# Fetching the next short group's row numbers and tokens one slot earlier in the expert stage of an attention and mixture-of-experts kernel

## The chip, the cores and the metric

The program runs on one core of a Trainium2 chip. The metric is device microseconds of one execution. Launches are timed singly; the kernel before was run three times. Beside them one execution was taken by the hardware profiler, and all rows below are from that one.

## The reference, cut to what matters

Three blocks run one after the other: attention with a learned position bias, a token and channel mixer, and a mixture of eight experts in which every token goes to one expert. Only the last block is touched.

```python
# x: [2, 576, 512] after the first two blocks; 8 experts; F = 1024
logits = x @ w_gate
e = argmax(logits) where the local gate is low (or at token 0), else the expert of the token before
p = softmax(logits)
h = maximum(x[b, s] @ w1[e], 0.0)          # w1[e]: 512 x 1024
out[b, s] = p[e] * (h @ w2[e])             # w2[e]: 1024 x 512
```

## The kernel before, in words

The 1152 tokens are sorted by expert on the chip. For each expert, rows of a table in HBM (`meta`) hold the row number of a token and its weight p. The tokens of an expert are worked in full slots of 128 (8 slots, t = 0 to 7) and what is left over, at most 32 tokens, in a short group (`little`, k = 0 to 3). A full slot does its two matrix products in three passes of float32r halves (`mm1`, `mm2`, line 743), for which the weights, loaded as float32 into `raw`, are split into a high part by ScalarE (a cast, line 1327) and a low part by VectorE or GpSimd (line 1328); of every four chunks the last one's low part is GpSimd's. A short group does the same with plain float32 matmuls of 32 columns against its own copies of the weights (`lw1`, `lw2`).

The short group k is worked between the steps of slots 2k and 2k+1, by a table of parts that `beside_slots` (lines 1506 to 1522) fills and `run` calls: its token transpose (`little_T`, line 1431) at the "top" of slot 2k, its first product (`little_mm1`, line 1441) at the end of slot 2k, its second transpose (line 1450) in the middle of slot 2k+1, its second product (line 1460) at the end of slot 2k+1. "Middle" is after the first half of the slot's `mm2`, the token transpose of slot t+2 (`x_T`, line 1335), the last two weight splits of slot t+2's `w1` and the issue of the weights of slot t+3. "Top" is in the loop's next turn, between the two halves of the next slot's `mm1`.

What one fetch for a short group, `little_tokens(k)`, issues, in order:

- on ScalarE's queue, a register load of the group's first row and a DMA (line 1400) of 32 rows of `meta`, repeated four times over the partitions, into `lmt` (line 1400). For k = 0 this is on SyncE's queue;
- on GpSimd, a tensor_scalar (line 1402) that makes four addresses of each row number (`lat`), which waits for `lmt`;
- on GpSimd, an indirect DMA (line 1404) that gathers the tokens' 128-element quarters from `x2d` into `lxt`, which waits for `lat`.

`lmt`, `lat` and `lxt` have two buffers each, so groups k and k+1 have different ones. `little_T` waits for `lxt`. All engines take their instructions in order; SyncE issues all weight loads, ScalarE the fetches for full slots from t = 3 on (`mt`, line 1291), GpSimd the gathers (line 1298) and the scatters of results (lines 1383 and 1464). Weight loads of a full slot carry a condition and move nothing where the expert is the one of the slot before.

Of the kernel before, what the change touches and what calls it, by code (L numbers as in the profile page):

```python
# [1219 lines left out]
class Experts:  # L1220
# [285 lines left out]
    def beside_slots(self):  # L1506

        parts = {}
        add = lambda t, where, *what: parts.setdefault((t, where), []).append(what)
        for k in range(NLITTLE):  # L1510
            t = 2 * k
            add(t, "top", self.little_T, k)
            add(t, "end", self.little_mm1, k)
            add(t + 1, "mid", self.little_hT, k)
            add(t + 1, "end", self.little_mm2, k)
            if k + 1 < NLITTLE:
                add(t + 1, "mid", self.little_tokens, k + 1, 1)

                for a in range(2):
                    add(t + 1 + a, "first", self.little_weights, k + 1, a, 0)  # L1520
                    add(t + 1 + a, "second", self.little_weights, k + 1, a, 1)
        return parts
# [156 lines left out]
```

## Time and profile before

| | |
|---|---|
| median of three runs | 623.33 us (621.42 to 626.04) |
| the profiled execution: its own time | 625.4 us |
| its span, first to last instruction | 623.6 us |
| time around the span | 1.8 us |
| PE busy | 564.0 us, 90% of the span |
| DVE, ACT, POOL busy | 379.3, 330.9, 236.2 us |
| mean granted TensorE clock | 0.961 |

The expert stage is the stretch from about 468 us to the end. The rows below are times of the profiled execution from the start of its span. PE is TensorE's matmul, PEld its weight load, DVE VectorE, ACT ScalarE, POOL GpSimd, SP SyncE; a "q" behind a name is the engine's sequencer (register loads, waits, DMA issues).

### The profile page before, as it was taken

What the parts mean: (1) busy time and instruction counts of PE and PEld (TensorE: products, weight loads), DVE (VectorE), ACT (ScalarE), POOL (GpSimd) and SP (SyncE); (2) the same over time, 40 slices, a digit from 0 to 9 for tenths busy, and PEclk for the clock granted to TensorE, in tenths of its full rate; (3) what the DMA queues carried; (4) which work ended last, traced back from release to release, by engine and by line L of the source; (5) the groups of instructions that cost most, each with busy time, mean ns of one, the idle gap of its engine ahead of it and who ended that gap; (6) DMA issues with size and microseconds to landing.
All of it is one profiled execution on the core that took longest, in us unless ns stands there. A gap on an engine that the chain in (4) does not pass through costs nothing.

```text
span 623.6 us, 11964 instructions
## 1 busy us (share of the span) xinstructions
PE 564.0 (90%) x4306; PEld 445.7 (71%) x4306; DVE 379.3 (61%) x891; ACT 330.9 (53%) x603; POOL 236.2 (38%) x230
## 2 busy tenths in 40 slices
PE   7699799898999999897889999999989998969693
PEld 3367577666777887796569988988767776857572
DVE  6689488688886764999982412536640345636340
ACT  4578587877896872345442211215222465747360
POOL 4667375455653450344440020030023334553331
PEclk8989899999999999999999999999989998979897
DMA  7997889799676321355511000026008933577640
GB/s 156 138 161 128 129 162 152 130 147 155 127 112 128 86 75 60 112 163 169 174 63 52 1 18 27 8 68 255 34 1 273 383 129 127 153 258 234 213 151 13
DMA packets 72110, 79.90 MB, mean 128 GB/s; under 512 B 36822, under 2 KB 51420, under 8 KB 72044
## 3 DMA queue, kind: packets, MB, share of 16 engines
q1 hardware_dynamic: 67276, 73.72, 49.6%
q0 software_dynamic: 2176, 5.26, 2.5%
q8 instruction: 36, 0.59, 0.4%
q10 hardware_dynamic: 2592, 0.09, 0.3%
q14 instruction: 30, 0.25, 0.2%
HBM read 72.08 MB, written 5.34 MB: 124 GB/s over the span
## 4 chain that ended last, share of the span: by engine, by line
PE 49%; issue 14%; DMA 13%; DVE 13%; ACT 5%; POOL 2%; SPq 2%; ACTq 1%; POOLq 0%; DVEq 0%
PE ph L743 12%; PE po L743 10%; DMA bias<-ev 8%; PE py L743 5%; PE tp L424 4%; PE ps L499 4%; PE ps L359 3%; DVE raw L727 3%; DMA lmt<-meta 2%; DMA lxt<-x2d,lat 2%; PE tp L410 2%; DVE wf L729 2%; ACT t L340 2%; PE tp L1364 2%; DVE t L337 1%
## 5 line engine op out<-in xcount | busy, mean ns | idle before, releaser
L743 PE MATMUL po<-cw,h 128*128 128x512 f32 x324 | 82.9, 402 | 5.5 <-POOL cw L735 4.9
L489 POOL TENSOR_SCALAR hd<-tabs,sc,negb 128x576 f32<-128x576 f32 x32 | 76.3, 2388 | 5.3 <-PE tp L440 1.8
L743 PEld LDWEIGHTS po<-cw,h 128*128 128x128 f32 x324 | 58.6, 188 | 22.6 <-POOL cw L735 9.0
L340 ACT ACTIVATE t<-t,st 128x576 f32<-128x576 f32 x72 | 55.4, 771 | 27.4 <-DVE st L337 27.1
L337 DVE CUSTOM_DVE_ANT_0 t<-ps,bias 128x576 f32<-128x576 f32 x72 | 52.5, 750 | 21.7 <-DMA bias<-ev 12.6
L359 PE MATMUL ps<-K,qt 128*128 128x288 f32 x320 | 55.9, 315 | 7.7 <-DVE qt L199 3.9
L424 PE MATMUL tp<-pt,v 128*64 128x128 f32 x800 | 54.7, 282 | 0.8 <-DVE K L272 0.8
L1328 DVE TENSOR_TENSOR big<-raw,big 128x1024 fp32r<-128x1024 f32 x30 | 37.5, 1272 | 29.4 <-ACT big L1327 29.2
L1106 POOL DMA_INDIRECT meta<-tokid,posi x10 | 10.0, 997 | 116.2 <-DVE tokid L1103 109.4
L499 PE MATMUL ps<-hd,wblk 128*32 128x288 f32 x576 | 47.3, 439 | 7.3 <-DVE st L337 5.9
L359 PEld LDWEIGHTS ps<-K,qt 128*128 128x128 f32 x320 | 46.1, 195 | 10.5 <-ACT ev L502 4.5
L424 PEld LDWEIGHTS tp<-pt,v 128*64 128x64 f32 x800 | 44.7, 139 | 8.5 <-issue 5.0
L743 PE MATMUL py<-big,hT 128*128 128x512 f32 x184 | 47.9, 400 | 0.0
L1327 ACT CAST big<-raw 128x1024 fp32r<-128x1024 f32 x44 | 44.2, 1052 | 3.0 <-issue 1.9
L743 PE MATMUL ph<-big,xT 128*128 128x512 f32 x168 | 44.3, 412 | 0.0
L743 PE MATMUL ph<-uT,big 128*128 128x384 f32 x216 | 40.6, 339 | 3.2 <-ACT big L734 1.8
L743 PE MATMUL po<-uT,big 128*128 128x384 f32 x216 | 41.3, 341 | 1.9 <-POOL big L735 1.9
L489 DVE TENSOR_SCALAR hd<-tabs,sc,negb 128x576 f32<-128x576 f32 x69 | 41.4, 629 | 1.0 <-PE ps L499 0.8
L1328 POOL TENSOR_TENSOR big<-raw,big 128x1024 fp32r<-128x1024 f32 x10 | 25.9, 2595 | 39.0 <-ACT big L1327 39.0
L743 PEld LDWEIGHTS ph<-uT,big 128*128 128x128 f32 x216 | 37.4, 188 | 4.6 <-ACT big L734 2.2
L743 PEld LDWEIGHTS po<-uT,big 128*128 128x128 f32 x216 | 37.2, 188 | 3.6 <-POOL big L735 2.9
L743 PEld LDWEIGHTS py<-big,hT 128*128 128x128 f32 x184 | 33.8, 188 | 8.2 <-issue 0.6
(279 smaller groups left out, 1086.3 us busy)
## 6 DMA issues: line engine op xcount, KB each, us to landing
raw<-in_moe_w_dram SPq DMA_DIRECT2D x48, 512.0 KB
raw<-in_moe_w_ch_dram SPq DMA_DIRECT2D x24, 512.0 KB
bias<-ev SPq DMA_DIRECT2D x32, 288.0 KB
qt<-qs SPq DMA_DIRECT2D x64, 128.0 KB
lw<-in_moe_w_dram SPq DMA_DIRECT2D x16, 512.0 KB
big<-in_moe_w_dram SPq DMA_DIRECT2D x8, 512.0 KB
lw<-in_moe_w_dram SPq DMA_DIRECT2D x16, 256.0 KB
big<-in_moe_w_dram SPq DMA_DIRECT2D x16, 256.0 KB
```

The lines of the kernel that those rows point to most:

```text
L337: nc.vector.tensor_tensor_reduce(t.rearrange("p (a j) -> p a j", a=2), ps[:, :, 0:HALF], bs.rearrange("p (a j) -> p a j", a=2), op0=ALU.ad ...
L340: nc.scalar.activation(t, t, AF.Exp, bias=st[:, j:j + 1], scale=-1.0, accum_out=st[:, 2 + j:3 + j])
L359: nc.tensor.matmul(ps[:, hf, 0:HALF], lhsT=qt[:, j], rhs=K[k][:, hf * HALF:(hf + 1) * HALF], start=j == pairs[0][0], stop=j == pairs[-1][0])
L410: nc.tensor.transpose(tp[:, 128 * j:128 * j + 128], tt[:, o:o + 128], ident)
L424: nc.tensor.matmul(po[64 * h:64 * h + 64, 0:128], lhsT=lhsT, rhs=rhs, start=j == 0, stop=j == 4)
L489: eng.tensor_scalar(hd[:, qq], Lt[:, o:o + S], sc[:, c], negb, ALU.mult, ALU.max)
L499: nc.tensor.matmul(ps[32 * qq:32 * qq + 32, hf, 0:HALF], lhsT=wblk, rhs=hd[:, qq, hf * HALF:(hf + 1) * HALF], start=True, stop=True)
L727: nc.vector.scalar_tensor_tensor(hi, hi, -2 ** 31, lo, ALU.bitwise_and, ALU.bitwise_or)
L729: nc.vector.scalar_tensor_tensor(dst.bitcast(I32), dst.bitcast(I32), 3, hi, ALU.logical_shift_left, ALU.bitwise_or)
L743: nc.tensor.matmul(out, lhsT=lhs[a], rhs=rhs[b], start=first and i == 0, stop=last and i == 2)
L1327: nc.scalar.copy(hi, raw)
L1328: (nc.gpsimd if c == 3 and t else nc.vector).tensor_tensor(lo, raw, hi.bitcast(F32), ALU.subtract)
```

## The change

The call that fetches for group k+1 is put into the middle of slot 2k in place of the middle of slot 2k+1. The function itself, its queues and its buffers are as they were. Three fetches are concerned, for k+1 = 1, 2, 3; the one for group 0 stands elsewhere.

```diff
         for k in range(NLITTLE):
             t = 2 * k
...
             add(t + 1, "mid", self.little_hT, k)
             add(t + 1, "end", self.little_mm2, k)
             if k + 1 < NLITTLE:
-                add(t + 1, "mid", self.little_tokens, k + 1, 1)
+                add(t, "mid", self.little_tokens, k + 1, 1)
 
                 for a in range(2):
                     add(t + 1 + a, "first", self.little_weights, k + 1, a, 0)
                     add(t + 1 + a, "second", self.little_weights, k + 1, a, 1)
```

## Rows read from the trace of the kernel before

**Rows 1.** Timeline of PE: start, length (us), what, and idle time before it.
```profile
516.99 0.44 PE L1431 MATMUL tp<-ident,lxt 128*128 128x128 f32 x1 [3.25 <-DMA lxt<-x2d,lat]
...
540.06 3.05 PE L743 MATMUL py<-big,hT 128*128 128x512 f32 x12
...
553.72 0.45 PE L1431 MATMUL tp<-ident,lxt 128*128 128x128 f32 x1 [5.74 <-DMA lxt<-x2d,lat]
...
565.31 1.93 PE L1441 MATMUL tp<-lw,lxT 128*32 128x256 f32 x32
...
590.84 0.45 PE L1431 MATMUL tp<-ident,lxt 128*128 128x128 f32 x1 [5.78 <-DMA lxt<-x2d,lat]
```

**Rows 2.** Chain that ended last, in order of time: start, length, what.
```profile
484.33 0.87 PE tp L1364 x8
485.21 2.80 PE ph L743 x12
...
511.56 5.30 DMA lxt<-x2d,lat
...
516.99 0.44 PE tp L1431
517.43 1.71 PE tp L1364 x8
519.14 3.13 PE ph L743 x12
...
541.07 5.74 DMA lmt<-meta
...
547.75 5.83 DMA lxt<-x2d,lat
...
555.87 3.49 PE ph L743 x12
...
578.45 8.57 DMA lmt<-meta
...
592.99 3.68 PE ph L743 x12
```

**Rows 3.** Windows: busy time of each engine, then granted clock, DMA share, GB/s.
```profile
516.99:519.00 2.01, 2.01 (x10) 2.01 (x11) 0.35 (x2) 0.59 (x1) 0.00 (x0) 0.50 0.39 130
```

**Rows 4.** Tile view of lxt: its gathers, from issue to landing.
```profile
DMA to landing us min/median/max: 2.7/5.6/7.3
```

**Rows 5.** Timeline of ACT, slots 0, 1, 2, 4 and 5.
```profile
491.77 2.00 ACT L1327 CAST big<-raw 128x1024 fp32r<-128x1024 f32 x2
...
494.11 0.69 ACT L1382 ACTIVATE y<-py,mt 128x512 f32<-128x512 f32 x1 [0.34 <-PE py L743]
...
499.40 1.07 ACT L1366 CAST hT<-tp 128x512 fp32r<-128x512 f32 x2 [3.01 <-PE tp L1364]
...
526.03 2.00 ACT L1327 CAST big<-raw 128x1024 fp32r<-128x1024 f32 x2
...
563.10 1.05 ACT L1327 CAST big<-raw 128x1024 fp32r<-128x1024 f32 x1
...
577.67 1.05 ACT L1327 CAST big<-raw 128x1024 fp32r<-128x1024 f32 x1
```

**Rows 6.** Windows of 2 us in slots 0 and 4, columns as in rows 3.
```profile
492.00:494.00 2.00, 2.00 (x9) 1.32 (x8) 1.75 (x2) 1.77 (x2) 0.14 (x1) 1.00 1.05 385
...
556.00:558.00 2.00, 2.00 (x7) 1.55 (x7) 1.59 (x3) 2.00 (x3) 0.00 (x0) 0.68 0.50 200
```

**Rows 7.** Timeline of POOL, slots 2 to 4.
```profile
536.71 2.85 POOL L1328 TENSOR_TENSOR big<-raw,big 128x1024 fp32r<-128x1024 f32 x1 [0.51 <-ACT big L1327]
...
546.97 0.26 POOL L1402 TENSOR_SCALAR lat<-lmt,block 128x1 int32<-128x1 int32 x1 [1.22 <-DMA lmt<-meta]
...
552.62 1.05 POOL L1298 DMA_INDIRECT xt<-x2d,mt  x1 [0.30 <-issue]
```

**Rows 8.** Waits of SP's queue from 465 us on: total us, times, longest.
```profile
SPq L1312 <- DMA lmt<-meta: 7.3, 2, 5.5
```

## The prediction

> **What bounds the kernel now.** I read three views of the stage that the change touches, in this order. First the chain of work that ended last, from 480 us on: it runs along TensorE through the full slots, but three times it leaves TensorE, goes through ScalarE's queue, the fetch into `lmt`, GpSimd's `lat` and the gather into `lxt`, and comes back at line 1431, the token transpose of a short group [rows 2]. That is what a fetch on the critical path looks like: both DMAs stand in the chain with their full length, 5.74 and 8.57 us for two of the `lmt` fetches, 5.30 and 5.83 us for two of the gathers. Second the timeline of PE: in the whole expert stage TensorE is idle before three instructions only that matter, the transposes of groups 1, 2 and 3, for 3.25, 5.74 and 5.78 us, each time until `lxt` lands [rows 1]. Group 0, fetched long before, has no such wait. Third the windows: after the wait the granted clock is 0.50, TensorE's 1.2 GHz level, in the two microseconds behind the transpose [rows 3], though TensorE had run at 1.00 (2.4 GHz) up to the wait. So each wait costs twice, once as idle time and once as slow matmuls behind it.
>
> **The sum.** The idle time: 3.25 + 5.74 + 5.78 = 14.77 us [rows 1]. The slow matmuls: undisturbed, in slot 0, the eight transposes of `h` take 0.87 us, so 0.11 us each, and the twelve matmuls behind them 2.80 us [rows 2]. Behind the first wait, the short group's transpose takes 0.44, the eight 1.71 and the twelve 3.13 us [rows 2]: (0.44 - 0.11) + (1.71 - 0.87) + (3.13 - 2.80) = 1.50 us. Behind the second and third the transposes repeat the pattern (the single one 0.45, rows 1), and the twelve take 3.49 and 3.68 us: 1.18 + 0.69 = 1.87 and 1.18 + 0.88 = 2.06 us. Together 5.43 us, and with the idle time 20.2 us. All of it lies on TensorE's path, which has no other idle time in the stage to absorb it. From the profiled execution's own 625.4 us this leaves 605.2; that execution was 2.1 us above the median of the runs shown, so beside the median of 623.33 the same sum gives 603.1 us.
>
> **Does the fetch land in time from its new place?** Nothing is removed or added; three fetches are moved some 14 us forward in time. In slot 0 the new place on ScalarE's queue is beside the two casts that begin at 491.77; in slots 2 and 4 the like casts begin at 526.03 and 563.10 [rows 5]. In the old place of slot 5 the issue came 0.78 us after the first of the casts beside it (577.67, rows 5, and 578.45, rows 2), so I put the new ones at about 492.6, 526.8 and 563.9. With the longest `lmt` fetch seen, 8.57 us [rows 2], 0.8 us for `lat` and the gap behind it (546.97 to the gather's 547.75, rows 7 and 2) and the longest gather, 7.3 us [rows 4], `lxt` is there 16.7 us later, at 509.3, 543.5 and 580.6. TensorE comes to the transposes at 513.7, 548.0 and 585.1, which are the starts in rows 1 less the idle times. Even with the longest of everything some 4.4 us are left each time. Earlier waits that vanish move fetch and need together, so these margins stand.
>
> The three new places differ in what else is on the DMA engines. In slot 0 they are full (share 1.05 at 492 to 494, rows 6), with group 0's own second weights. That is no better than where the 8.57 us fetch stood. The Trainium skill, DMA: Bandwidth & Descriptors, "Issuing engines are not separate DMA queues", speaks against the move here: transfers from different issuing engines run on the same 16 DMA engines and interleave, so ScalarE's small fetch doesn't escape SyncE's weights by having its own queue. The trace agrees, with 1 KB in 8.57 us; by the rule the sum loses at most the first place's 4.75 us, and by the row's margin nothing.
>
> **What the moved instructions now stand in front of.** ScalarE's queue: the register load and the issue stand in front of the slot's result copy, group k's relu and then the `hT` casts of the next slot, the first of them that TensorE waits for. In slot 0 the split casts end at 493.8 and the `hT` casts begin at 499.40, 5.6 us later; the copy takes 0.69 of it [rows 5], and the relu, a half as wide tile, less. That leaves over 4 us; I count one for the load and the issue (an assumption, no row has them alone) and 3.2 us for any hold. What could hold the issue: the trace shows SyncE's weight issue, line 1312, twice waiting for `lmt` to land (7.3 us, the longest 5.5, rows 8), though no data passes between them, so the DMAs of both queues seem to wait for one another's completions in some turn. No row shows ScalarE held so. I bound the hold by 0 and by 5.5 us and take it as under 3.2, nearer to the rows of ScalarE that show none; at 5.5 it would cost 2.3 us of TensorE, in slot 0. A gain on ScalarE from the place that is left, the middle of slot 2k+1, I exclude: TensorE has no idle time there to give back, as its only waits are those of rows 1.
>
> GpSimd's queue: `lat` now waits in front of the scatter and the next full slot's gather of slot 2k, and behind those stands the next weight split. In slot 2 that split starts at 536.71, 0.51 us after the queue came free, and ends 2.85 us later [rows 7]; its low part is read by the seventh of `mm2`'s eight steps; the second four start at 540.06 [rows 1], so it is needed about 541.5, and 1.9 us are to spare. From `lat` to the end of the slot's gather GpSimd took 546.97 to 553.67, 6.7 us, with one scatter of 1.3 us that isn't in the new place [rows 7]: 5.4 without it. So `lmt` has until about 533.2, that is 6.4 us after issue; beyond that each microsecond is one of TensorE's. The two lengths of rows 2 lie on both sides: the cost here is 0 to 2.2 us. I take 0: DMA engines have only 1 MB of the short group's weights before them queued there (four chunks of 128 x 512), less than in front of the 8.57 us fetch, which stood beside a slot's and a group's weights.
>
> SyncE's queue isn't passed by any instruction, but a weight issue may wait for `lmt` [rows 8]. The tightest transfer behind it is the second half of group 2's first weights, which have landed when the DMA engines fall quiet, about 557 (share 0.50 at 556 to 558, rows 6). It is used from the second half of line 1441's group, which starts at 565.31 [rows 1] and would start 7.6 us earlier: 557.7, and 0.9 us for its first half gives 558.6. So 1.6 us are to spare, and this becomes the next thing late if the weights keep their old time. One of the old `lmt` fetches (541.07 to 546.8) lay in front of just these weights, so they should come earlier rather than later. At worst they wait a full 5.5 us [rows 8], 3.9 beyond the room; at best nothing is gained, since TensorE doesn't wait for them now. I take 0.
>
> **The rivals.** (a) A new wait takes part of the gain: ScalarE held in slot 0, GpSimd's split in slot 2, or group 2's weights in slot 4. By the bounds above 2.3, 2.2 and 3.9 us, and behind each some 1.5 us of slow matmuls as behind the 3.25 us wait: a single one gives 605 to 608.5, all of them 616. For it: margins of 1.6 and 1.9 us. Against: the trace of slots 1, 3, 5, which run without waits at the same loads.
>
> (b) The fetch still doesn't come in time: its two transfers take longer beside the weights of slots 0, 2 and 4 than any row shows. From the issue they may take 16.7 + 4.4 = 21.1 us at no cost; each microsecond more is idle time at line 1431 again, and some 27 us each time leave all of the three waits. Then it is 617 to 625. For it: the full DMA engines of slot 0 [rows 6]. Against: slots 2 and 4 have no such queue, and 16.7 is the sum of the longest of everything already.
>
> (c) Slower: ScalarE, held at the issue, holds the `hT` casts and with them TensorE, at all three places. The point from which this decides: a hold of more than the room of 3.2 us costs TensorE one for one. To cancel 20.2 us it must be about 10 us each time; at 14 us each it is 3 x 10.8 = 32.4 less the gain, 636 us. For it: ScalarE works in order and the DMA engines are full in slot 0 [rows 6]. Against it: the longest wait of rows 8 is half of what it needs.
>
> **How the numbers follow.** Forecast, all three waits gone and at most 3 us given back: 0.76, time 603.1. (a) above that: 0.15. (b): 0.06. (c): 0.03. The range: low end, the forecast from the fastest run, 621.4 - 20.2 = 601.2, less 1 us for the spread of the runs afterwards, 600.2; high end 610, a single new wait at its full price with a microsecond for the spread of the runs. That leaves out the worst of (a), and (b) and (c), together with what is below some 0.15. Within 1%, about what a measurement of this kernel can tell from no change, is 617.1 to 629.6: most of (b) and a third of (c), 0.06. Faster by more: 0.92, the forecast, (a) and a corner of (b). Slower by more: 0.02.
>
> **What would show it.** In the profile of the changed kernel the idle time before line 1431 should be gone for all three groups, the eight transposes behind it take 0.87 us, and the granted clock be 1.00 from slot 0 to the last; the two DMAs should be gone from the chain. `lat` should run about 15 us before the transpose that needs it. It is wrong if line 1366 waits for ScalarE in slot 1, if line 743 waits for GpSimd's split in slot 3, or if line 1441 waits for `lw` in slot 4; or if line 1431 still has idle time before it.

## The result, and the profile after

The changed kernel takes 603.43 us (median of 4 runs, 600.01 to 604.61), the kernel before 624.68 beside it (4 runs, 621.42 to 627.35). The ratio is 0.9653, with a 95% interval of 0.9589 to 0.9718: by it 21.7 us faster, between 17.6 and 25.7. The forecast was 603.1.

The profiled execution took 602.8 us with a span of 601.0; before, 625.4 and 623.6. Of these 22.6 us, 2.1 were there before the change could act: the transpose of group 0 starts at 481.95 instead of 484.06, a difference between two executions. From that transpose to the end it is 119.05 us instead of 139.54, so 20.5 us come from the stage. The sum said 20.2.

The timeline of PE after the change, columns as in [rows 1]; a row with idle time before it would have a bracket:

```profile
511.47 0.27 PE L1431 MATMUL tp<-ident,lxt 128*128 128x128 f32 x1
511.57 1.03 PE L1364 MATMUL tp<-ident,h 128*128 128x128 f32 x8
512.37 3.04 PE L743 MATMUL ph<-big,xT 128*128 128x512 f32 x12
...
540.98 0.27 PE L1431 MATMUL tp<-ident,lxt 128*128 128x128 f32 x1
...
570.45 0.27 PE L1431 MATMUL tp<-ident,lxt 128*128 128x128 f32 x1
```

The three brackets of [rows 1] are gone, and no other has come; the list of PE's waits from 475 us to the end of its work is empty. The chain, which counts the part of each piece that doesn't overlap the next, has the eight transposes at 0.87 and the twelve matmuls at 2.80 us behind the group's transpose, where it had 1.71 and 3.13 [rows 2]:

```profile
511.63 0.11 PE tp L1431
511.74 0.87 PE tp L1364 x8
512.61 2.80 PE ph L743 x12
```

The granted clock in the two microseconds from the eight transposes on is 1.00, the upper level, now (windows of groups 1 and 3, columns as in [rows 3], where it was 0.50; the clock is the third column from the end):

```profile
511.57:513.60 2.03, 2.03 (x15) 1.82 (x14) 2.03 (x4) 1.75 (x4) 0.20 (x1) 1.00 0.97 296
...
570.55:572.60 2.05, 2.05 (x16) 1.83 (x15) 1.83 (x4) 1.41 (x3) 0.55 (x1) 1.00 1.01 404
```

Where the moved instructions run now, on ACT and on POOL (timelines):

```profile
491.64 1.11 ACTq L1400 DMA_DIRECT2D lmt<-meta  x1
492.87 0.69 ACT L1382 ACTIVATE y<-py,mt 128x512 f32<-128x512 f32 x1 [1.22 <-DMA lmt<-meta]
...
519.64 1.08 ACTq L1400 DMA_DIRECT2D lmt<-meta  x1
...
549.12 1.05 ACTq L1400 DMA_DIRECT2D lmt<-meta  x1
```

```profile
496.26 0.27 POOL L1402 TENSOR_SCALAR lat<-lmt,block 128x1 int32<-128x1 int32 x1 [2.06 <-DMA lmt<-meta]
497.03 1.05 POOL L1404 DMA_INDIRECT lxt<-x2d,lat  x1 [0.51 <-POOL lat L1402]
...
525.27 0.27 POOL L1402 TENSOR_SCALAR lat<-lmt,block 128x1 int32<-128x1 int32 x1 [0.92 <-DMA lmt<-meta]
525.99 2.01 POOL L1404 DMA_INDIRECT lxt<-x2d,lat  x1 [0.46 <-POOL lat L1402]
...
529.62 1.80 POOL L1298 DMA_INDIRECT xt<-x2d,mt  x1 [0.31 <-issue]
531.45 2.42 POOL L1328 TENSOR_TENSOR big<-raw,big 128x1024 fp32r<-128x1024 f32 x1
...
553.33 2.18 POOL L1402 TENSOR_SCALAR lat<-lmt,block 128x1 int32<-128x1 int32 x1
555.78 1.76 POOL L1404 DMA_INDIRECT lxt<-x2d,lat  x1 [0.27 <-POOL lat L1402]
```

The gathers start 14 to 15 us before the transposes that need them (497.03, 525.99 and 555.78 against 511.47, 540.98 and 570.45). The waits did not vanish, they went where nobody is kept by them: GpSimd still waits for `lmt` 2.06 and 0.92 us, and ScalarE is idle for 1.22 us before its result copy in slot 0, where it was idle for 0.34 [rows 5]. The view names the fetch for that; what kept ScalarE's queue is the issue of the fetch, from 491.64 to 492.75.

### The profile page after: what moved, and what is told of

Its sections match the earlier page's. It is cut to its first block, busy times and chain, and to the rows that moved or that the text cites. A ratio compares the mean times of both kernels' runs of the same rounds, so it can differ in the third digit from the quotient of the medians.

```text
span 601.0 us, 11964 instructions
## 1 busy us (share of the span) xinstructions
PE 557.9 (93%) x4306; PEld 442.2 (74%) x4306; DVE 384.4 (64%) x891; ACT 329.7 (55%) x603; POOL 242.5 (40%) x230
## 4 chain that ended last, share of the span: by engine, by line
PE 55%; issue 14%; DVE 13%; DMA 8%; ACT 3%; POOL 3%; SPq 1%; ACTq 0%; POOLq 0%; DVEq 0%
PE ph L743 13%; PE po L743 10%; DMA bias<-ev 6%; PE py L743 6%; PE tp L424 5%; PE ps L359 4%; PE ps L499 4%; PE tp L410 3%; DVE raw L727 3%; DVE wf L729 2%; DVE K L272 1%; PE tp L743 1%; DVE hd L489 1%; DVE t L337 1%; ACT t L340 1%
## 5 line engine op out<-in xcount | busy, mean ns | idle before, releaser
L743 PEld LDWEIGHTS po<-cw,h 128*128 128x128 f32 x324 | 58.6, 188 | 22.6 <-POOL cw L735 9.1
L1328 DVE TENSOR_TENSOR big<-raw,big 128x1024 fp32r<-128x1024 f32 x30 | 43.3, 1468 | 19.3 <-ACT big L1327 19.1
L424 PE MATMUL tp<-pt,v 128*64 128x128 f32 x800 | 52.8, 278 | 0.8 <-DVE K L272 0.8
L424 PEld LDWEIGHTS tp<-pt,v 128*64 128x64 f32 x800 | 43.1, 136 | 8.1 <-issue 5.3
L743 PE MATMUL ph<-big,xT 128*128 128x512 f32 x168 | 42.8, 402 | 0.0
L486 ACT ACTIVATE hd<-tabs,b1c,sc 128x576 f32<-128x576 f32 x43 | 36.9, 866 | 3.9 <-DVE sc L457 3.8
```

The source lines that it names most:

```text
L424: nc.tensor.matmul(po[64 * h:64 * h + 64, 0:128], lhsT=lhsT, rhs=rhs, start=j == 0, stop=j == 4)
L486: nc.scalar.activation(hd[:, qq], Lt[:, o:o + S], AF.Relu, bias=b1c, scale=sc[:, c])
L743: nc.tensor.matmul(out, lhsT=lhs[a], rhs=rhs[b], start=first and i == 0, stop=last and i == 2)
L1328: (nc.gpsimd if c == 3 and t else nc.vector).tensor_tensor(lo, raw, hi.bitcast(F32), ALU.subtract)
```

## The experiments

Eight more kernels ran; each ratio is to the kernel before on the same chip. Where "the stage" is given in microseconds, it is the time from the transpose of group 0 to the end of the span in the profiled execution: 139.54 us in the kernel before, 119.05 in the changed one. The first two ask whether the three waits are independent and as large as the sum says.

**The first group's fetch alone.**

```diff
-                add(t, "mid", self.little_tokens, k + 1, 1)
+                add(t if k == 0 else t + 1, "mid", self.little_tokens, k + 1, 1)
```

> Only the fetch for group 1 is moved, those for groups 2 and 3 stand where they were before. Theory (each wait at line 1431 costs its own idle time and the slow matmuls behind it, and the three are independent): the wait of group 1 is gone, those of groups 2 and 3 stay near 5.7 us each; 4.75 us faster than the kernel before, ratio 0.992. Rival (the gain came from the DMAs and their semaphores as a whole, so that the fetches help or hurt one another): something else than 4.75, down to nothing.

619.84 us, ratio 0.9945 (0.9917 to 0.9972): 3.4 us faster, between 1.7 and 5.2, with the 4.75 in it; the stage takes 135.2 us, 4.4 less than before. The wait of group 1 is gone, the other two stand:

```profile
510.46 0.27 PE L1431 MATMUL tp<-ident,lxt 128*128 128x128 f32 x1
...
546.48 0.45 PE L1431 MATMUL tp<-ident,lxt 128*128 128x128 f32 x1 [6.34 <-DMA lxt<-x2d,lat]
...
582.77 0.45 PE L1431 MATMUL tp<-ident,lxt 128*128 128x128 f32 x1 [5.13 <-DMA lxt<-x2d,lat]
```

Their sum, 11.47 us, is that of before, 11.52 [rows 1]: the fetches don't help one another.

**The last group's fetch alone.**

```diff
-                add(t, "mid", self.little_tokens, k + 1, 1)
+                add(t if k == 2 else t + 1, "mid", self.little_tokens, k + 1, 1)
```

> Only the fetch for group 3 is moved. Theory: the wait of group 3 is gone, those of groups 1 and 2 stay near 3.3 and 5.7 us; 7.8 us faster than before, ratio 0.987. Rival as for the first group alone: another size, and the two parts don't add up with group 2's 7.6 to the 20 to 21 us of the whole change.

616.49 us, ratio 0.9877 (0.9838 to 0.9915): 7.7 us faster, where 7.8 was expected. Group 3 has no wait, groups 1 and 2 have 3.68 and 6.22 us. The two parts and the 7.6 us that were worked out for group 2 make 18.7 us, inside the interval of the whole change. The rival of both runs finds no support in this; group 2's fetch was not run alone.

**The row numbers early, the gather where it was.** The chain of before gives the `lmt` fetch its full 5.74 and 8.57 us [rows 2]. If that is a price, moving this fetch alone takes most of the gain. `little_tokens` is cut in two here: `little_rows` has the register load and the DMA into `lmt`, `little_gather` has `lat` and the gather.

```diff
-                add(t, "mid", self.little_tokens, k + 1, 1)
+                add(t, "mid", self.little_rows, k + 1, 1)
+                add(t + 1, "mid", self.little_gather, k + 1)
```

> The row numbers (lmt, on ScalarE's queue) are fetched at the new place for all three groups; lat and the gather of the tokens stay at the old place on GpSimd. Theory (in the old place lat was held by GpSimd's weight split in front of it as much as by lmt, and the gather alone takes 5 to 6 us): group 1 gains nothing, since lat ran right behind the split there; group 2 about 1 us; group 3 between 1.5 and 4.6. In all 3 to 6 us faster than before, some 618 to 621, and waits remain at all three groups. Rival (the row numbers' fetch, 5.74 and 8.57 us in the chain, is what made the fetch late): most of the gain is there, 606 to 611.

620.94 us, ratio 0.9947 (0.9920 to 0.9973): 3.3 us faster, between 1.7 and 5.0. The waits are 3.04, 4.73 and 4.25 us, so 0.2, 1.0 and 1.5 less than before. The timeline of POOL shows what holds `lat` (line 1410 here) when `lmt` is long there; groups 2 and 3 have the same picture:

```profile
504.96 2.47 POOL L1328 TENSOR_TENSOR big<-raw,big 128x1024 fp32r<-128x1024 f32 x1 [6.85 <-ACT big L1327]
507.54 0.27 POOL L1410 TENSOR_SCALAR lat<-lmt,block 128x1 int32<-128x1 int32 x1
508.08 1.05 POOL L1412 DMA_INDIRECT lxt<-x2d,lat  x1 [0.27 <-POOL lat L1410]
```

Two lengths stand behind each other in the old place, GpSimd's weight split and `lmt`, and taking away one uncovers the other. Then the gather follows, 5 to 6 us by itself. The fetch was late as a whole, not through its longest piece.

**The old kernel with the wait filled.** Is the slow clock behind a wait a price of its own?

```diff
         nc, L = self.nc, self.LT[k]
+        if 0 < k < NLITTLE:
+            fill, t = self.tr(), 2 * k + 1
+            for _ in range((14, 24, 24)[k - 1]):
+                nc.tensor.matmul(fill, lhsT=self.XT[t][0][:, 0:128], rhs=self.W[t, 0, 2][0][:, 0:512], start=True, stop=True)
         tp = self.tr()
```

> The kernel before, with 14, 24 and 24 matmuls of 128x128 by 128x512 (read by nobody) put in front of the transposes of groups 1, 2 and 3 on TensorE, about as long as the idle times there. Theory (a wait costs the idle time and then the slow clock): the granted clock stays at 1.00 behind the waits, the eight transposes take 0.87 us instead of 1.71, and the kernel is up to 5.4 us faster than before though it does more work; 619 to 621, less what the filling overshoots the wait. Rival (the slow matmuls behind a wait cost nothing in the end, since ScalarE's and VectorE's splits end last there): same as before, 624, or slower.

620.2 us, ratio 0.9968 (0.9920 to 1.0015): the time alone decides nothing. The profile does, group by group. PE's timeline (the group's transpose is line 1435 here):

```profile
509.95 3.43 PE L1433 MATMUL tp<-big,xT 128*128 128x512 f32 x14
513.35 1.04 PE L1364 MATMUL tp<-ident,h 128*128 128x128 f32 x8
514.14 3.05 PE L743 MATMUL ph<-big,xT 128*128 128x512 f32 x12
...
542.76 5.77 PE L1433 MATMUL tp<-own,xT 128*128 128x512 f32 x24
549.32 0.30 PE L1435 MATMUL tp<-ident,lxt 128*128 128x128 f32 x1 [0.78 <-DMA lxt<-x2d,lat]
549.45 1.04 PE L1364 MATMUL tp<-ident,h 128*128 128x128 f32 x8
...
578.81 5.76 PE L1433 MATMUL tp<-big,xT 128*128 128x512 f32 x24
586.75 0.30 PE L1435 MATMUL tp<-ident,lxt 128*128 128x128 f32 x1 [2.17 <-DMA lxt<-x2d,lat]
586.89 1.44 PE L1364 MATMUL tp<-ident,h 128*128 128x128 f32 x8
587.98 4.31 PE L743 MATMUL ph<-big,xT 128*128 128x512 f32 x12
```

Behind the first two fillings the granted clock stays at 1.00 and the eight transposes take the 1.04 us of an undisturbed slot (1.92 in this view before). From the end of slot 2's first product half to the end of the twelve matmuls the chain has 7.06 us (510.12 to 517.18) instead of 8.53 (513.74 to 522.27): 1.47 less, where the sum put 1.50 on the slow matmuls. Group 2 can be read in the chain too: from its transpose to the end of the twelve matmuls it has 3.96 us (549.32 to 553.28) instead of 5.65 (553.72 to 559.36), so 1.69 less, where the sum put 1.87. The gain is still there, 1.68 us, when TensorE is done with its work before the transpose of group 3 (549.32 to 578.98 in the timeline, instead of 553.72 to 585.06). For group 3 it couldn't be shown: `lmt` took 10.90 us there (the chain: "572.06 10.90"), the wait outlasted the filling by 2.17 us, and the clock fell. Longer waits are why the time hardly moved: 6.6 and 7.9 us from the first filling matmul to the transposes of groups 2 and 3, against idle times of 5.74 and 5.78 before. So the theory is shown for two waits of three.

**The changed kernel, with the old fetch repeated.** Perhaps what helped was that the old place was cleared.

```diff
                 add(t, "mid", self.little_tokens, k + 1, 1)
+                add(t + 1, "mid", self.little_again, k + 1)
```

`little_again` issues the three instructions once more into tiles of its own, with rows half as long in the gather.

> The changed kernel, and at the old place a second fetch of the same rows for every group into tiles that nobody reads (the same three instructions on the same queues; the gather brings rows half as long). Theory (all that counts is when lxt lands): as fast as the changed kernel, 603, no wait at line 1431. Rival (the gain is the relief of ScalarE's and GpSimd's queues and of the DMAs' semaphores at the old place): most of the gain is lost, 615 to 624.

606.03 us, ratio 0.9718 (0.9673 to 0.9762). Line 1431 (1437 here) has no wait, and 18 of the 21 us stay: the rival falls. By the medians it is 2 to 3 us slower than the changed kernel, and than the kernel with the fetch at the top of slot 2k+1 (below), which ran beside it. In the profiled execution the stage takes 123.2 us, 4.1 more than in the changed kernel, and 3.9 of these come after group 3's transpose. There the second `lat` keeps GpSimd and with it a weight split that `mm2` needs, in slot 6:

```profile
574.29 0.27 POOL L1402 TENSOR_SCALAR latagain<-lmtagain,block 128x1 int32<-128x1 int32 x1 [6.48 <-DMA raw<-in_moe_w_dram]
...
579.33 2.37 POOL L1328 TENSOR_TENSOR own<-raw,big 128x1024 fp32r<-128x1024 f32 x1
```

The view puts GpSimd's 6.48 us down to a weight transfer; `latagain` reads `lmtagain` alone, whose fetch ScalarE issued at 563.68. PE waits for the split:

```profile
581.75 0.80 PE L743 MATMUL py<-own,hT 128*128 128x512 f32 x1 [2.27 <-POOL own L1328]
```

The rest of what is lost is slow matmuls: from 581.75 to 584.00 the granted clock is 0.50. This is the mechanism of rival (a), GpSimd's queue, met in a kernel that brings it about.

**How far the fetch may move.** Two runs put it later, at the top of slot 2k+1, and earlier, at the top of slot 2k. Measured from the transpose of group k, the issue of `lmt` comes 4 to 6 us later in the one and 9 to 10 us earlier in the other (a slot is about 14.7 us).

```diff
-                add(t, "mid", self.little_tokens, k + 1, 1)
+                add(t + 1, "top", self.little_tokens, k + 1, 1)
```

> The whole fetch stands at the top of slot 2k+1, between the new place and the old one. Theory: ScalarE, idle before the hT casts of that slot, comes to it some 4 to 6 us later than in the new place, lxt still lands 2 to 4 us before line 1431 needs it, and no wait is there; but lat, held until lmt lands, now stands directly in front of the weight split of slots 3 and 5 on GpSimd, and line 743 waits for that low part by 0 to 2 us in slot 3; 603 to 607. Rival (the fetch needs the whole of the slot that it was given): a part of the waits at line 1431 is back, 608 to 618.

603.91 us, ratio 0.9656 (0.9614 to 0.9698), the same as the change. No wait at line 1431; in slot 3 GpSimd's split runs right behind the gather, from 534.12 to 536.78, and the last matmuls of `mm2` start with its end (the twelve take 3.48 us in PE's timeline instead of 3.04). The rival, that the whole slot is needed, falls.

```diff
-                add(t, "mid", self.little_tokens, k + 1, 1)
+                add(t, "top", self.little_tokens, k + 1, 1)
```

> The whole fetch stands at the top of slot 2k, earlier than the change by most of a slot. Theory: nothing is left to gain, since TensorE has no wait in the stage of the changed kernel; 603, and lxt lands some 20 us ahead. Rival (a fetch so early stands in front of other work, lat behind the scatter of the group before): slower than the change by up to 5 us.

605.92 us, ratio 0.9688 (0.9651 to 0.9726), 2.0 us above the run at the top of slot 2k+1 beside it; the times of the two overlap (603.16 to 606.81 and 600.64 to 604.61), so it is the profile that decides. There the theory, that nothing changes any more, was too simple and the rival right: the stage takes 124.8 us, 5.8 more than in the changed kernel. POOL in slot 4:

```profile
544.50 1.04 POOL L1298 DMA_INDIRECT xt<-x2d,mt  x1 [4.81 <-DMA mt<-meta]
545.63 1.64 POOL L1402 TENSOR_SCALAR lat<-lmt,block 128x1 int32<-128x1 int32 x1
547.54 1.06 POOL L1404 DMA_INDIRECT lxt<-x2d,lat  x1 [0.27 <-PE py L743]
548.63 2.35 POOL L1328 TENSOR_TENSOR big<-raw,big 128x1024 fp32r<-128x1024 f32 x1
```

PE behind it:

```profile
551.04 2.50 PE L743 MATMUL py<-big,hT 128*128 128x512 f32 x5 [3.04 <-POOL big L1328]
553.47 3.58 PE L1441 MATMUL tp<-lw,lxT 128*32 128x256 f32 x32
```

The full slot's gather waits 4.81 us for its row numbers; `lat` and the gather for the group come between it and the split, which takes 3.0 us more; PE waits 3.04 us for the split, and the matmuls behind the wait are slow (line 1441 takes 3.58 us instead of 1.93). It is not the scatter of the group before, which the rival named.

**ScalarE held.** The prediction gave ScalarE's queue 3.2 us of room at the new place.

```diff
+                add(t, "mid", self.hold)
                 add(t, "mid", self.little_tokens, k + 1, 1)
```

`hold` copies 64 columns of the identity 24 times into a tile that nobody reads.

> The changed kernel with 24 small copies on ScalarE (64 columns, read by nobody) in front of the fetch in slots 0, 2 and 4, which hold the queue there for some 4.5 to 7 us each time. Theory (ScalarE has a room of 3.2 us there, beyond which the hT casts are late and TensorE waits one for one): TensorE waits before mm2 of slots 1, 3 and 5 or before the next slot for 1.3 to 3.8 us each time, 607 to 616. Rival (ScalarE has more room than that, since the casts behind can be late without TensorE waiting): 603 to 605.

618.88 us, ratio 0.9897 (0.9842 to 0.9953). The 24 copies take 6.6 us each time (one row of ACT's timeline: 491.79, 6.61). PE's waits:

```profile
502.43 3.33 PE L743 MATMUL py<-big,hT 128*128 128x512 f32 x12 [1.70 <-ACT hT L1366]
535.70 0.50 PE L743 MATMUL py<-big,hT 128*128 128x512 f32 x1 [3.25 <-ACT hT L1366]
537.26 1.22 PE L743 MATMUL py<-big,hT 128*128 128x512 f32 x2 [0.83 <-DVE hT L1367]
559.94 1.44 PE L743 MATMUL py<-big,hT 128*128 128x512 f32 x5 [0.39 <-POOL big L1328]
571.99 0.73 PE L743 MATMUL py<-big,hT 128*128 128x512 f32 x2 [2.08 <-ACT hT L1366]
573.58 4.15 PE L743 MATMUL py<-big,hT 128*128 128x512 f32 x10 [0.86 <-DVE hT L1367]
```

Slots 1, 3 and 5 lose 1.70, 4.08 and 2.94 us, so of the 6.6 us some 4.9, 2.5 and 3.7 were covered by the room in slots 0, 2 and 4, if what is past the room is lost one for one. For slot 0 3.2 was worked out. The waits make 9.1 us, but the stage takes 134.7 us, 15.7 more than in the changed kernel. The other 6.6 are slow matmuls in the main (the last row above has ten in 4.15 us; in an undisturbed slot this view has twelve in 2.95), which the expectation had left out; hence 619 and not 607 to 616.

## Why the prediction was right

**The sum.** Each of its terms was met, and the two profiles show it piece by piece. From one group's transpose to the next by the starts in the chain, and from the last one to the end of the span, the kernel before took 32.76, 36.73, 37.12 and 32.76 us, the changed one 29.52, 29.51, 29.47 and 30.39. The differences are 3.24, 7.22, 7.65 and 2.37 us. In the sum the same pieces, each with a group's idle time and the slow matmuls of the group before it, are 3.25, 5.74 + 1.50 = 7.24, 5.78 + 1.87 = 7.65 and 2.06. That the clock was a price by itself the filled kernel shows, with 1.47 and 1.69 us for the first two waits where 1.50 and 1.87 stood; for the third there is only the changed kernel. Moved alone, groups 1 and 3 gave 3.4 (1.7 to 5.2) and 7.7 us (5.3 to 10.1), where 4.75 and 7.84 stood, and the waits left standing beside them changed by less than a microsecond in total (11.47 us for 11.52, 9.90 for 8.99).

The stage gained 20.5 us, where the sum had 20.2. Of the 21.7 us that the ratio gives one can't tell more: its interval is 8 us wide. That 603.43 us lies 0.3 from the forecast is partly luck, since the kernel before, run beside the changed one, had a median 1.35 us above the 623.33 from which the forecast started.

**Whether the fetch lands in time.** It does in all three groups, with more to spare than the 4.4 us that the longest rows left: `lat` ran 4.6 and 5.6 us after the issue of `lmt` in slots 0 and 2 (491.64 to 496.26 and 519.64 to 525.27), and 4.2 us after it in slot 4, straight behind GpSimd's split. From the starts of the gathers even the 7.3 us of [rows 4] would leave some 7 us. The full DMA engines of slot 0 didn't lengthen the fetch beyond the rows. The Trainium skill, DMA: Bandwidth & Descriptors, "Issuing engines are not separate DMA queues", states that transfers issued by ScalarE run on the same 16 DMA engines as SyncE's. Nothing in the traces speaks against it, but how busy the engines are doesn't set the length of the fetch by itself: their share was 0.84 over the 4.6 us of slot 0, and 0.71 over the 10.90 us of the filled kernel, the longest fetch of all, whose cause stays open. With the fetch 4 to 6 us later line 1431 still has no wait, so the margin is real.

**ScalarE.** The hold that the prediction bounded by 0 and 5.5 us, with no row that showed one, was there in slot 0. The register move of the fetch and its issue (tile view of `lmt`: shortest, median and longest in ns, first and last start):

```profile
L1400 ACTq MOVE lmt<-meta x3: 29/29/29, 489.9 to 549.1; - x3
L1400 ACTq DMA_DIRECT2D lmt<-meta x3: 1055/1083/1108, 491.6 to 549.1; - x3
```

In slot 4 the issue follows the move at once; in slot 0 1.7 us lie between them (2.3 us at the same place in the kernel with the first group's fetch alone, 488.9 to 491.2). In the trace the semaphore that this issue waits for was last raised at 491.62, just before it, by the landing of a weight transfer of SyncE's (`lw`), so ScalarE waited for a transfer of another queue that it has no data from, as SyncE does in [rows 8]. The 1.7 us lie inside the room of 3.2, and the issue took 1.1 us, where one was assumed. The `hT` casts of slot 1 still have 3.01 us of idle time before them, as in [rows 5].

The room itself was worked out for slot 0 alone, to the start of the `hT` casts. `mm2`, which reads them, starts at 500.33, 2.0 us after the casts end, and this fits the 4.9 us that the held kernel finds there. In slot 2, where ScalarE's casts for the weight splits reach up to the `hT` casts without a gap (to 526.76, and 526.77), it finds only 2.5, less than the 3.2: the room is tightest at a place for which the prediction had not worked it out. Past the room come waits and slow matmuls, as rival (c) said; that the wait is one for one isn't shown, since the room is worked out from the waits.

**GpSimd.** This was the closest call. In slot 2 the split followed the gather without a gap (531.42 to 531.45, a queue that is just not late), and ended at 533.87; by the prediction's count `mm2` needs it some 1.4 us after its second half starts at 533.19. The 1.9 us to spare of the old timing had become 0.7. One term was too small: from `lat` to the end of the slot's gather it was 6.2 us (525.27 to 531.42), not 5.4, since the slot's gather took 1.80 us to issue and not 1.05 (the last section shows beside what); `lmt`, which came 0.8 us before its limit of 6.4, and a shorter split, 2.42 us for 2.85, made up for it. The cost of 0 was right, but in the runs with one more `lat` in front of a split, or an earlier one (repeated, still earlier), PE waited 2.27 and 3.04 us for just this, and the stage took 4.1 and 5.8 us more.

**Group 2's weights and SyncE.** No wait at line 1441 is in PE's list, and SyncE waited for `lmt` 2.1 us in two waits, 1.6 the longest, without anybody late behind it. The room of 1.6 us that the prediction called the tightest was not tested by a run of its own.

**One reading has to be put right.** The prediction showed the fetch as critical by the two DMAs that stand in the chain with their full length. The sum didn't use these lengths, and rightly: with the `lmt` fetch, the longer one in group 3, taken out of the old place, 3.3 us were gained. A chain names what came last, and what comes second may be right behind it.

## What to carry to other kernels

Price a late transfer by the wait of the engine that needs it plus the slow matmuls behind the wait, not by the transfer's length in the chain: several late pieces in a row hide one another. Move a small fetch with all its queue entries, early enough that the longest latencies seen still fit, and no further; on an in-order queue every microsecond that it waits in front of other work may be one of theirs. When the move is done, the next thing to look at is the queue in which it now stands, here GpSimd, where one entry in the wrong place made TensorE wait 2.3 and 3.0 us in two experiments, and the slow matmuls behind the wait came on top.

## What the runs showed of the hardware that was not expected

With nothing but three small fetches moved, VectorE's splits took longer in the profiled execution. The groups of VectorE's line 1328, before and after (line, engine, operation, count, busy us and mean ns, idle time before):

```profile
L1328 DVE TENSOR_TENSOR big<-raw,big 128x1024 fp32r<-128x1024 f32 x30 | 37.5, 1272 | 29.4 <-ACT big L1327 29.2
```

```profile
L1328 DVE TENSOR_TENSOR big<-raw,big 128x1024 fp32r<-128x1024 f32 x30 | 43.3, 1468 | 19.3 <-ACT big L1327 19.1
...
546.65 4.35 DVE L1328 TENSOR_TENSOR big<-raw,big 128x1024 fp32r<-128x1024 f32 x2 [1.22 <-ACT big L1327]
```

The pair at 546.65 took 4.35 us; an undisturbed pair takes 2.36. GpSimd's own split ran beside it from 546.37 to 548.77, and took 2.40 us. On the other side, GpSimd's `lat`, 0.27 us elsewhere, took 2.18 us at 553.33, beside three VectorE splits that stretch from 551.52 to 556.59. The Trainium skill, SBUF — State Buffer, "Who interferes with whom", has VectorE operations with two SBUF inputs contend with GpSimd's reads, and whoever issues second wait for the first to finish. The trace agrees with it here, in both directions. GpSimd's gathers and scatters show the same: from 465 us on, all seven of the changed kernel whose issue took over 1.3 us (1.63 to 2.07, where 1.0 is usual) began while a split of line 1328, with two inputs in SBUF, ran on VectorE, and were longer by about what was left of it; three that began beside line 1367, which reads one of its inputs from PSUM, took 1.01 to 1.02 us. No run was made to separate this from other causes. It cost nothing here: PE's list has no wait.

TensorE's clock: behind an idle time of 2.17 us (filled kernel, group 3) the granted clock was 0.62 in the next two microseconds, and behind 2.27 us (repeated fetch, slot 6) 0.50, as behind the 3.25 us of [rows 1]; behind 0.78 us (filled kernel, group 2) and 1.70 us (held kernel, slot 1) it stayed at 1.00.
